# Local attention scores of 64 queries by 96 keys, and tiles placed at multiples of 512 bytes, in a fused sparse-attention and feed-forward kernel

## The chip, the cores and the metric

The kernel runs on one core of a Trainium2 chip. The metric is device time in microseconds for one execution of the whole program. Engines are named as in the profile: PE (TensorE), DVE (VectorE), ACT (ScalarE), POOL (GpSimd) and SP (SyncE, which issues DMAs).

## The reference

Inputs are q, k and v of 8 batches, 8 heads, 576 tokens and 64 dimensions, and two weight matrices, all float32. Heads 0 to 3 attend locally: a query sees itself and the 31 tokens before it. Heads 4 to 7 attend with stride 32: a query sees the earlier tokens at the same place modulo 32. The result goes through a feed-forward layer.

```python
scores = scale * np.matmul(q, k.transpose(0, 1, 3, 2))
mask_local = (rel >= 0) & (rel < stride)          # rel = query - key, stride = 32
mask_strided = (rel >= 0) & (pos[None, :] % stride == pos[:, None] % stride)
scores = np.where(masks[None, :, :, :], scores, -1000000000.0)
attn = softmax(scores)                            # over the keys
x = (attn @ v) as 4608 tokens of 512
h = x @ w_in                                      # 512 by 2048
out = (h * sigmoid(h)) @ w_out                    # 2048 by 512
```

## The kernel before

**The feed-forward part.** Tokens go in nine blocks of 512, the hidden dimension in 16 chunks of 128. Every float32 matrix product is made of three products of float32r values: each operand is split into a high and a low part (`xhi` and `xlo`, `ghi` and `glo`, and two weight tiles), and high by high, high by low and low by high are summed. So a chunk of the first layer (`hidden`, L594) is 12 matmul instructions of 128 x 128 by 512 columns with `w` stationary and `x` moving, and a chunk of the second (`output`, L658) is 12 with `g` stationary and the weights moving: 2 x 9 x 16 x 12 = 3,456 in all. Between the layers `silu` makes th (ACT, L604), the gate (DVE, L626), `ghi` (L634) and `glo` (L638).

The weights stay in SBUF. Of the second layer, chunks 0 to 6 lie in tiles named `w`; chunks 7 and 8 are lent the tiles `k2` and `k3`, chunks 9 to 11 the tiles `v2` to `v5`, and chunks 12 to 15 the `stage` tiles, once the first batch no longer needs these.

**The attention part.** Each batch has three local groups (12 tiles of 32 queries for each of two heads) and three strided ones (8, 8 and 6 tiles). Steps of a group: `scores` (PE, L378), `peak` (DVE, L396: scale, mask and running minimum into `sm`), `weigh` (ACT, L413: exponential and its sum), `total` (DVE, L428 and L429), `scale` (DVE, L432), `turn_by_blocks` (DVE, L454 and L457: transposes of 32 x 32 blocks from `sm` to `pt`), `values_by_halves` (PE, L497) and `done_by_halves` (ACT, L509 and L537). A local tile's scores are a product of 32 queries by 64 keys; a float32 product is two PE instructions.

**Order.** Up to the end of the first block everything follows an order written out by hand (`PLAN`). Each engine runs its instructions in that order. From then on a loop goes over chunks: `hidden` of one chunk, `silu`, and `output` of the chunk before. Three times per block (chunks 1, 6 and 11) `products` puts a burst on PE: local scores of a later group, local values, strided values, strided scores of a later group. Behind it stand the outstanding `output`, the local group's `weigh`, `normalize` and transposes, and three quarters of the strided `weigh`; the rest follows one and two chunks later. After a burst no output is outstanding, so the next chunk's gate must be done when the `hidden` behind it ends. Groups are counted over the batches, six a batch, local ones at even numbers from batch 1 on.

**Memory.** Tiles of the pool `const` come first in each partition, in the order in which they are made; the compiled program rounds each up to 32 bytes. `pad0` ends at byte 1,536, so the `v` tiles, `k` tiles and `ident` begin at multiples of 512. Then come four masks of 288 bytes, `ones` (8 bytes, rounded to 32) and `pad1` (376, rounded to 384): `stage0` begins at byte 38,432, which is 75 x 512 + 32, and everything behind it (stages, `w`, `xb`, `sm`, `pt`, `x`, `th`, `g`) is 32 bytes past a multiple too, but for the small `sums`.

POOL makes `ident` and the masks at the start, in program order.

Of the kernel before, what the change touches and what calls it, by code (L numbers as in the profile page):

```python
# [13 lines left out]
F32 = mybir.dt.float32  # L14
# [9 lines left out]
B, H, S, D = 8, 8, 576, 64  # L24
DM, DFF = 512, 2048
STRIDE = 32
NJ = S // STRIDE
NP = H // 2
P = 128
# [13 lines left out]


KW = 64
SEQ = 3 * NJ
QW = 512
HALF = SEQ // 2
# [16 lines left out]
class Group:  # L65
    def __init__(self, local, first, count):
        self.local, self.first, self.count = local, first, count
        self.rows = STRIDE if local else KW
        self.per = P // self.rows
        self.n = count // self.per  # L70
        self.q0 = [self.rows * t for t in range(count)]
        half = S // STRIDE
        gap = [STRIDE if local and first < half <= first + t else 0 for t in range(count)]
        self.k0 = [(STRIDE if local else SEQ) * t + g for t, g in enumerate(gap)]
        self.nq = self.q0[-1] + self.rows
        self.nk = self.k0[-1] + KW

        self.at = [(t % self.n, t // self.n) for t in range(count)]

        self.starts = [  # L80
            tuple(r for t, (at, r) in enumerate(self.at)
                  if at == c and local and (first + t) % half == 0)
            for c in range(self.n)
        ]
# [88 lines left out]
def sparse_attention_ffn(ctx: ExitStack, tc: tile.TileContext, kqt, vt, w_in, w_out, out):  # L173
    nc = tc.nc
    const = ctx.enter_context(tc.tile_pool(name="const", bufs=1))
# [26 lines left out]
    make_identity(nc, ident)  # L202


    def mask(name):
        m = const.tile([P, 72], F32, name=name)
        nc.gpsimd.memset(m, 0.0)
        return m

    def keep(m, p0, rows, shape, steps, base, channel):  # L210
        part = m[p0 : p0 + rows, : math.prod(shape)]
        nc.gpsimd.affine_select(
            out=part, in_=part, pattern=[[s, c] for s, c in zip(steps, shape)],
            base=base, channel_multiplier=channel, compare_op=ALU.is_ge, fill=NEG,
        )

    masks = {}
    m = mask("mask_local")
    for t in range(P // STRIDE):
        keep(m, t * STRIDE, STRIDE, [KW], [1], -1, -1)  # L220
        keep(m, t * STRIDE, STRIDE, [KW], [-1], STRIDE, 1)
    masks[True, ()] = m
    for starts in sorted({s for g in GROUPS for s in g.starts if s}):
        first = const.tile([P, 72], F32, name="mask_first" + "".join(map(str, starts)))
        nc.gpsimd.tensor_copy(out=first, in_=m)
        for t in starts:
            keep(first, t * STRIDE, STRIDE, [KW], [1], -STRIDE, 0)
        masks[True, starts] = first
# [5 lines left out]
    masks[False, ()] = m  # L234
    ones = const.tile([P, 2], F32, name="ones")
    nc.gpsimd.memset(ones, 0.0)
    for h in range(2):
        nc.gpsimd.memset(ones[h * D : (h + 1) * D, h : h + 1], 1.0)
    const.tile([P, 94], F32, name="pad1")


    cuts = ((0, NFC), (0, 7, 9, 12, 14, NFC))
# [102 lines left out]
    class Attention:  # L345


        def __init__(self, b, at):
            self.b, self.at, self.gi = b, at, order_of(b)[at]
            self.by_blocks = b * NG + at >= TURNED  # L350
            self.g = g = GROUPS[self.gi]
            self.spread = b * NG + at in SPREAD
            self.sums_by_pe = self.spread and g.local and not self.by_blocks
            self.kbd, self.vbd = kbds[kbd_of(b, at)], vbds[vbd_of(b, at)]
            self.cols = g.n * P
            self.tiles = [
                (t, c, slice(r * g.rows, (r + 1) * g.rows))
                for t, (c, r) in sorted(enumerate(g.at), key=lambda tile: tile[1])
            ]


# [5 lines left out]

        def halves(self, banks):

            return [t.rearrange("p (c k) -> p c k", k=KW)[:, : self.g.n] for t in banks]  # L370

        def scores(self, banks=None):
            g, kbd = self.g, self.kbd
            self.pss = banks or [self.bank("pss") for _ in range(2)]
            for t, c, rows in self.tiles:
                for h in range(2):
                    at = slice(h * D, (h + 1) * D)
                    nc.tensor.matmul(  # L378
                        self.pss[h][rows, c * KW : (c + 1) * KW],
                        kbd[at, 1, g.q0[t] : g.q0[t] + g.rows],  # L380
                        kbd[at, 0, g.k0[t] : g.k0[t] + KW], start=True, stop=True,
                    )

        def peak(self):
            g = self.g
            s_ps = self.halves(self.pss)
            self.sm = att.tile([P, 512], F32, name="sm", bufs=3)
            self.s_sb = self.sm.rearrange("p (c h k) -> p c h k", h=2, k=KW)[:, : g.n]
# [3 lines left out]
            self.inv = rsum.unsqueeze(3).broadcast_to([P, g.n, 2, KW])  # L392
            for c in range(g.n):
                for h in range(2):

                    nc.vector.tensor_tensor_reduce(  # L396
                        out=s_sb[:, c, h], in0=s_ps[h][:, c], in1=masks[g.local, g.starts[c]][:, :KW],
                        scale=-SCALE, scalar=BIG, op0=ALU.add, op1=ALU.min,
                        accum_out=peaks[:, c, h : h + 1],
                    )  # L400

        def lessen(self):
            peaks = self.peaks.unsqueeze(3).broadcast_to([P, self.g.n, 2, KW])
            nc.gpsimd.tensor_sub(self.s_sb, self.s_sb, peaks)

        def weigh(self, cs=None):
# [38 lines left out]
        def turn_by_blocks(self):  # L445

            n, size = self.g.n, P // STRIDE
            pt = att.tile([P, 512], F32, name="pt")[:, : self.cols]  # L450
            self.pt = pt = pt.rearrange("k (s c h q) -> k s c h q", s=2, h=2, q=STRIDE)
            src = self.sm[:, : self.cols].rearrange("p (c h s k) -> p s c h k", h=2, s=2, k=STRIDE)
            for s in range(2):
                nc.vector.transpose(out=pt[:, s], in_=src[:, s])  # L454
            for r in range(size):
                rows, to = (slice(i * STRIDE, (i + 1) * STRIDE) for i in (r, r ^ 1))
                nc.vector.transpose(out=pt[to, r % 2], in_=src[rows, 1 - r % 2])  # L457

        def values(self):
            g, pt, vbd = self.g, self.pt, self.vbd  # L460
# [26 lines left out]
        def values_by_halves(self, banks):  # L487
            g, pt, vbd = self.g, self.pt, self.vbd
            self.pso = banks
            half, size = g.count // 2, STRIDE if g.local else SEQ  # L490
            for i in range(half):
                for p in range(2):
                    c, r = g.at[p * half + i]
# [552 lines left out]
```

## Time and profile before

| | |
|---|---|
| median of 3 runs | 879.7 us (879.64 to 879.81) |
| the profiled execution | 879.54 us |
| its span | 877.6 us |
| PE busy | 869.5 us, 7217 matmul instructions |
| DVE, ACT, POOL busy | 509.4, 315.5, 37.2 us |
| granted PE clock | 1.0 of full speed |

The span runs from the first to the last instruction that the profiler saw; the time of the execution has 1.9 us more around it. An engine's share of busy time is a mean over stretches with different limits. Matmuls overlap in their pipeline, so the duration of one (some 390 ns for 512 columns) is longer than its distance to the next.

### The profile page before, as it was taken

To read this page: it belongs to the slowest core of one execution; us is meant where nothing else is said; L and a number is where in the kernel's file an instruction comes from. 1 tells how busy PE (TensorE), PEld (TensorE's weight loads), DVE (VectorE), ACT (ScalarE), POOL (GpSimd) and SP (SyncE) were. 2 spreads that over 40 slices of the span, in tenths; PEclk is the share of its full clock that TensorE was granted. 3 is DMA by queue.
4 is the path that set the end of the run, shared out by engine and by line. 5 is a ranking of instruction groups with operands and counts; after the bars stand their busy time and mean duration, and the time that the engine had idled before them with its cause. 6 is when DMAs were issued, how large, how long until landed. Compare 5 with 4: busy or idle time off the path is not lost.

```text
span 877.6 us, 18034 instructions
## 1 busy us (share of the span) xinstructions
PE 869.5 (99%) x7217; PEld 709.1 (81%) x7217; DVE 509.4 (58%) x1602; ACT 315.5 (36%) x1070; POOL 37.2 (4%) x55
## 2 busy tenths in 40 slices
PE   9999999999999999999999999999999999999998
PEld 6877788888878888888888888888888888888886
DVE  6999887448556646646645755664662533343333
ACT  7987763314412333333331441333331311131111
POOL 3123410000000000000000000000000000000000
PEclk9999999999999999999999999999999999999999
DMA  8976452202301212220320230221210000000001
GB/s 284 311 245 212 138 175 69 72 8 70 117 16 56 77 52 65 72 74 23 97 72 1 76 117 1 71 77 49 69 29 1 24 25 1 1 27 23 0 1 48
DMA packets 37044, 64.60 MB, mean 74 GB/s; under 512 B 2912, under 2 KB 23776, under 8 KB 36960
## 3 DMA queue, kind: packets, MB, share of 16 engines
q1 hardware_dynamic: 36144, 62.79, 21.9%
q8 instruction: 56, 0.92, 0.4%
q10 hardware_dynamic: 816, 0.66, 0.3%
q14 instruction: 28, 0.23, 0.1%
HBM read 54.00 MB, written 9.44 MB: 72 GB/s over the span
## 4 chain that ended last, share of the span: by engine, by line
PE 93%; DVE 2%; ACT 2%; DMA 1%; issue 1%; SPq 0%; POOL 0%; POOLq 0%; ACTq 0%; DVEq 0%
PE po L658 44%; PE ps L594 42%; PE ps L497 3%; PE ps L378 3%; PE ps L752 1%; DMA stage<-w_out 1%; DMA stage<-w_in 1%; ACT stage L265 1%; DVE stage L271 1%; ACT stage L260 0%; DVE glo L638 0%; DVE th L626 0%; ACT sm L413 0%; SPq L336 0%; DVE sm L396 0%
## 5 line engine op out<-in xcount | busy, mean ns | idle before, releaser
L594 PE MATMUL ps<-xhi,w 128*128 128x512 f32 x1152 | 377.2, 390 | 0.6 <-DVE th L626 0.6
L626 DVE SCALAR_TENSOR_TENSOR th<-th,ps 128x512 f32<-128x512 f32 (+1 forms) x147 | 99.2, 676 | 269.9 <-ACT th L604 269.8
L594 PEld LDWEIGHTS ps<-xhi,w 128*128 128x128 f32 x1152 | 216.2, 188 | 47.3 <-DVE th L626 0.9
L604 ACT ACTIVATE th<-ps 128x512 f32<-128x512 f32 (+1 forms) x147 | 86.6, 590 | 456.0 <-PE ps L594 453.3
L594 PE MATMUL ps<-xlo,w 128*128 128x512 f32 x576 | 224.5, 390 | 0.0
L658 PE MATMUL po<-w,ghi 128*128 128x512 f32 x504 | 157.1, 392 | 1.2 <-DVE sums L396 1.1
L594 PEld LDWEIGHTS ps<-xlo,w 128*128 128x128 f32 x576 | 108.1, 188 | 22.3
L658 PEld LDWEIGHTS po<-w,ghi 128*128 128x128 f32 x504 | 93.7, 188 | 21.2 <-issue 1.0
L413 ACT ACTIVATE sm<-sm,sums 128x64 f32<-128x64 f32 x320 | 106.4, 339 | 2.9 <-DVE sums L396 2.9
L638 DVE TENSOR_TENSOR glo<-th,ghi 128x512 fp32r<-128x512 f32 (+1 forms) x139 | 95.7, 688 | 11.9
L658 PE MATMUL po<-w,glo 128*128 128x512 f32 x252 | 98.4, 391 | 0.4 <-DVE glo L638 0.4
L658 PE MATMUL po<-stage,ghi 128*128 128x512 f32 x288 | 88.8, 389 | 0.0
L658 PE MATMUL po<-v,ghi 128*128 128x512 f32 x216 | 68.8, 400 | 0.0
L457 DVE STREAM_TRANSPOSE pt<-sm 32x192 f32<-32x192 f32 (+1 forms) x168 | 65.9, 392 | 3.0
L634 DVE CAST ghi<-th 128x512 fp32r<-128x512 f32 (+1 forms) x134 | 56.6, 422 | 12.9 <-PE po L658 1.3
L658 PEld LDWEIGHTS po<-stage,ghi 128*128 128x128 f32 x288 | 54.0, 188 | 11.2
L413 ACT ACTIVATION_READ_ACCUMULATOR sm<-sm,sums 128x1 f32 x320 | 61.7, 193 | 0.0
L658 PEld LDWEIGHTS po<-w,glo 128*128 128x128 f32 x252 | 47.3, 188 | 11.3 <-DVE glo L638 1.0
L658 PE MATMUL po<-stage,glo 128*128 128x512 f32 x144 | 56.0, 389 | 0.0
L658 PEld LDWEIGHTS po<-v,ghi 128*128 128x128 f32 x216 | 39.9, 188 | 9.3
L658 PE MATMUL po<-k,ghi 128*128 128x512 f32 x144 | 45.3, 396 | 0.0
L658 PE MATMUL po<-v,glo 128*128 128x512 f32 x108 | 42.7, 396 | 0.0
(75 smaller groups left out, 668.5 us busy)
## 6 DMA issues: line engine op xcount, KB each, us to landing
out<-stage SPq DMA_DIRECT2D x36, 256.0 KB, 2.1
v<-vt SPq DMA_DIRECT2D x21, 384.0 KB, 5.3
stage<-w_out SPq DMA_DIRECT2D x14, 512.0 KB, 4.1
k<-kqt SPq DMA_DIRECT2D x14, 512.0 KB, 5.2
stage<-w_in SPq DMA_DIRECT2D x12, 512.0 KB, 4.3
k<-kqt SPq DMA_DIRECT2D x14, 416.0 KB, 3.8
v<-vt SPq DMA_DIRECT2D x14, 256.0 KB, 5.2
k<-kqt SPq DMA_DIRECT2D x7, 448.0 KB, 4.1
```

The costliest lines, as they stand in the source:

```text
L265: nc.scalar.activation(out=lower, in_=lower.bitcast(U32), func=AF.Copy, scale=0.875 * 2.0**-29, bias=0.49)
L271: nc.vector.scalar_tensor_tensor(out=upper, in0=upper, scalar=3, in1=lower, op0=ALU.logical_shift_left, op1=ALU.bitwise_or,)
L378: nc.tensor.matmul(self.pss[h][rows, c * KW : (c + 1) * KW], kbd[at, 1, g.q0[t] : g.q0[t] + g.rows], kbd[at, 0, g.k0[t] : g.k0[t] + KW], s ...
L413: nc.scalar.activation(out=self.s_sb[:, c, h], in_=self.s_sb[:, c, h], func=AF.Exp, bias=self.peaks[:, c, h : h + 1], scale=-1.0, accum_ou ...
L457: nc.vector.transpose(out=pt[to, r % 2], in_=src[rows, 1 - r % 2])
L497: nc.tensor.matmul(self.pso[p][h * D : (h + 1) * D, i * size : (i + 1) * size], vbd[at, 2 * i + h], moved, start=True, stop=True,)
L594: nc.tensor.matmul(ph, weight(0, wi, fc)[:, cc * P : (cc + 1) * P], x[xi][cc], start=(cc, n) == (0, 0), stop=(cc, n) == (NP - 1, 2),)
L604: nc.scalar.activation(out=th[:, cols], in_=ph[:, cols], func=AF.Tanh, scale=0.5)
L626: nc.vector.scalar_tensor_tensor(out=th[:, cols], in0=th[:, cols], scalar=1.0, in1=ph[:, cols], op0=ALU.add, op1=ALU.mult,)
L634: copy[engine](out=g[0][:, cols], in_=th[:, cols])
L638: either[engine].tensor_sub(out=g[1][:, cols], in0=th[:, cols], in1=g[0][:, cols].bitcast(F32))
L658: nc.tensor.matmul(po[tt], g[gi][:, cols], weight(1, wi, fc), start=fc == 0 and n == 0, stop=fc == NFC - 1 and n == 2,)
```

## The change

Two things change. Groups from number 14 on (the second local group of batch 2 and all local groups after it) make their local scores in products of 64 queries by 96 keys: two neighbouring tiles share one product, whose keys are the block before the first, the first's own and the second's own. The tiles are laid out in pairs for that (`paired`), the masks have a form of 96 keys, `sm` has 640 columns, and the rows of `sm` hold 96 weights where they held 64; the transposes pick the two blocks of 32 that each tile needs. `values_by_halves` is as before but for the place of each tile. The PSUM bank shared by values and later scores is cut at column 192 for local groups. Second, `pad1` has 160 columns. By the same rounding, `stage0` then begins at byte 39,936, which is 78 x 512, and all tiles behind it begin at multiples of 512 (the `sums` at multiples of 128).

```diff
+WIDE = KW + STRIDE
+WIDE_FROM = 14
...
+        self.paired = [(t % (count // 2) // 2, 2 * (t // (count // 2)) + t % 2)
+                       for t in range(count)]
...
-    m = mask("mask_local")
-    for t in range(P // STRIDE):
-        keep(m, t * STRIDE, STRIDE, [KW], [1], -1, -1)
-        keep(m, t * STRIDE, STRIDE, [KW], [-1], STRIDE, 1)
-    masks[True, ()] = m
...
+    for wide, keys in ((False, KW), (True, WIDE)):
+        m = mask(f"mask_local{keys}", keys + 8)
+        for t in range(P // STRIDE):
+            ahead = STRIDE * (t % 2) if wide else 0
+            keep(m, t * STRIDE, STRIDE, [keys], [1], -1 - ahead, -1)
+            keep(m, t * STRIDE, STRIDE, [keys], [-1], STRIDE + ahead, 1)
+        masks[wide, ()] = m
+        some = {s for g in GROUPS for s in (g.paired_starts if wide else g.starts) if s}
+        for starts in sorted(some):
+            first = const.tile([P, keys + 8], F32, name=f"mask{keys}_" + "".join(map(str, starts)))
+            nc.gpsimd.tensor_copy(out=first, in_=m)
+            for t in starts:
+                keep(first, t * STRIDE, STRIDE, [keys], [1], -STRIDE, 0)
+            masks[wide, starts] = first
     m = mask("mask_strided")
...
-    const.tile([P, 94], F32, name="pad1")
+    const.tile([P, 160], F32, name="pad1")
...
+            self.wide = g.local and b * NG + at >= WIDE_FROM
+            self.at_of = g.paired if self.wide else g.at
+            self.keys = WIDE if self.wide else KW
...
+            if self.wide:
+                for t in (0, 6, 2, 8, 4, 10):
+                    c, r = self.at_of[t]
+                    rows = slice(r * STRIDE, (r + 2) * STRIDE)
+                    for h in range(2):
+                        at = slice(h * D, (h + 1) * D)
+                        nc.tensor.matmul(
+                            self.pss[h][rows, c * WIDE : (c + 1) * WIDE],
+                            kbd[at, 1, g.q0[t] : g.q0[t] + 2 * STRIDE],
+                            kbd[at, 0, g.k0[t] : g.k0[t] + WIDE], start=True, stop=True,
+                        )
+                return
...
-            self.sm = att.tile([P, 512], F32, name="sm", bufs=3)
+            self.sm = att.tile([P, 640], F32, name="sm", bufs=3)
...
+            blocks = self.keys // STRIDE
+            src = self.sm[:, : n * 2 * self.keys].rearrange(
+                "p (c h s k) -> p s c h k", h=2, s=blocks, k=STRIDE
+            )
             for s in range(2):
-                nc.vector.transpose(out=pt[:, s], in_=src[:, s])
+                nc.vector.transpose(out=pt[:, s], in_=src[:, s * (blocks - 1)])
...
-                nc.vector.transpose(out=pt[to, r % 2], in_=src[rows, 1 - r % 2])
+                nc.vector.transpose(out=pt[to, r % 2], in_=src[rows, 1 if self.wide else 1 - r % 2])
...
-            left, right = ([bank[:, at : at + 256] for bank in banks] for at in (0, 256))
+            cut = 192 if groups[i].g.local else 256
+            left, right = [bank[:, :cut] for bank in banks], [bank[:, cut:] for bank in banks]
```

## Rows read from the trace of the kernel before

**Rows 1.** The page: busy time by engine, and the chain's shares by line.
```profile
PE 869.5 (99%) x7217; PEld 709.1 (81%) x7217; DVE 509.4 (58%) x1602; ACT 315.5 (36%) x1070; POOL 37.2 (4%) x55
...
PE po L658 44%; PE ps L594 42%; PE ps L497 3%; PE ps L378 3%; PE ps L752 1%; DMA stage<-w_out 1%; DMA stage<-w_in 1%; ACT stage L265 1%; DVE stage L271 1%; ACT stage L260 0%; DVE glo L638 0%; DVE th L626 0%; ACT sm L413 0%; SPq L336 0%; DVE sm L396 0%
```

**Rows 2.** The chain of waits, 300 to 400 us: start us, us, work.
```profile
345.38 2.72 PE ps L594 x12
348.10 2.72 PE po L658 x12
...
366.98 2.80 PE po L658 x12
369.79 2.75 PE ps L594 x12
...
383.62 2.80 PE po L658 x12
```

**Rows 3.** Groups by shape: line, engine, tiles, count | busy us, mean ns | idle.
```profile
L658 PE MATMUL po<-w,ghi 128*128 128x512 f32 x504 | 157.1, 392 | 1.2 <-DVE sums L396 1.1
...
L658 PE MATMUL po<-stage,ghi 128*128 128x512 f32 x288 | 88.8, 389 | 0.0
L658 PE MATMUL po<-v,ghi 128*128 128x512 f32 x216 | 68.8, 400 | 0.0
...
L658 PE MATMUL po<-k,ghi 128*128 128x512 f32 x144 | 45.3, 396 | 0.0
```

**Rows 4.** PE's timeline over one burst: start us, us, work.
```profile
326.31 0.72 PE L378 MATMUL ps<-k 64*32 64x64 f32 x48
326.96 1.39 PE L497 MATMUL ps<-pt,v 64*64 64x32 f32 x80
328.17 0.66 PE L378 MATMUL ps<-k 64*64 64x64 f32 x32
328.75 0.72 PE L658 MATMUL po<-w,ghi 128*128 128x512 f32 x2
```

**Rows 5.** The chain of waits near the start.
```profile
11.71 0.33 PE po L438 x3
```

**Rows 6.** Groups by shape on ACT and DVE.
```profile
L413 ACT ACTIVATE sm<-sm,sums 128x64 f32<-128x64 f32 x320 | 106.4, 339 | 2.9 <-DVE sums L396 2.9
...
L432 DVE TENSOR_TENSOR sm<-sm,sums 128x384 f32<-128x384 f32 x27 | 17.2, 636 | 0.9
...
L432 DVE TENSOR_TENSOR sm<-sm,sums 128x512 f32<-128x512 f32 x13 | 9.0, 692 | 0.5
```

**Rows 7.** DVE's timeline behind the same burst.
```profile
332.17 0.56 DVE L432 TENSOR_TENSOR sm<-sm,sums 128x384 f32<-128x384 f32 x1
...
335.17 0.69 DVE L626 SCALAR_TENSOR_TENSOR th<-th,ps 128x512 f32<-128x512 f32 x1 [0.22 <-ACT th L604]
...
336.36 0.69 DVE L638 TENSOR_TENSOR glo<-th,ghi 128x512 fp32r<-128x512 f32 x1
```

**Rows 8.** PE's timeline where that output begins.
```profile
337.06 0.61 PE L658 MATMUL po<-w,ghi 128*128 128x512 f32 x2
337.51 0.39 PE L658 MATMUL po<-w,glo 128*128 128x512 f32 x1
```

**Rows 9.** POOL's timeline at the start.
```profile
1.02 0.29 POOL masks.py:199 TENSOR_SCALAR_AFFINE_SELECT ident<-ident 128x128 f32<-128x128 f32 x1
...
1.49 2.27 POOL L212 TENSOR_SCALAR_AFFINE_SELECT mask_local<-mask_local 32x64 f32<-32x64 f32 x8
3.82 0.24 POOL L225 COPY mask_first<-mask_local 128x72 f32<-128x72 f32 x1
...
4.32 0.23 POOL L225 COPY mask_first<-mask_local 128x72 f32<-128x72 f32 x1
...
5.14 2.46 POOL L212 TENSOR_SCALAR_AFFINE_SELECT mask_strided<-mask_strided 32x72 f32<-32x72 f32 x8
```

**Rows 10.** DVE's timeline at the first strided reduction.
```profile
11.00 0.22 DVE L396 CUSTOM_DVE_ANT_0 sm<-ps,mask_strided 128x64 f32<-128x64 f32 x1
```

More of the change, by code (lines that the diff above doesn't have):

```diff
@@ L78, in __init__ @@
         self.at = [(t % self.n, t // self.n) for t in range(count)]
[L80 to L84, printed above, removed]
+        self.paired = [(t % (count // 2) // 2, 2 * (t // (count // 2)) + t % 2)
+                       for t in range(count)]
+        self.starts, self.paired_starts = (
+            [tuple(r for t, (at, r) in enumerate(ats)
+                   if at == c and local and (first + t) % half == 0) for c in range(self.n)]
+            for ats in (self.at, self.paired)
+        )
 GROUPS = [Group(True, 12 * i, 12) for i in range(3)]
@@ L202, in sparse_attention_ffn, with mask @@
     make_identity(nc, ident)
-    def mask(name):
-        m = const.tile([P, 72], F32, name=name)
+    def mask(name, columns=72):
+        m = const.tile([P, columns], F32, name=name)
         nc.gpsimd.memset(m, 0.0)
@@ L217, in sparse_attention_ffn @@
     masks = {}
-    m = mask("mask_local")
-    for t in range(P // STRIDE):
-        keep(m, t * STRIDE, STRIDE, [KW], [1], -1, -1)
-        keep(m, t * STRIDE, STRIDE, [KW], [-1], STRIDE, 1)
-    masks[True, ()] = m
[L223 to L228, printed above, removed]
+    for wide, keys in ((False, KW), (True, WIDE)):
[12 more added lines that the diff above has]
+            masks[wide, starts] = first
     m = mask("mask_strided")
@@ L233, in sparse_attention_ffn @@
         keep(m, t * STRIDE, STRIDE, [4, NJ], [NJ, 0], NJ - 1 - q0, -1)
-    masks[False, ()] = m
+    masks[None, ()] = m
     ones = const.tile([P, 2], F32, name="ones")
@@ L355, in __init__ @@
             self.cols = g.n * P
+            self.wide = g.local and b * NG + at >= WIDE_FROM
+            self.at_of = g.paired if self.wide else g.at
+            self.keys = WIDE if self.wide else KW
+            starts = g.paired_starts if self.wide else g.starts
+            self.masks = [masks[self.wide if g.local else None, some] for some in starts]
             self.tiles = [
                 (t, c, slice(r * g.rows, (r + 1) * g.rows))
-                for t, (c, r) in sorted(enumerate(g.at), key=lambda tile: tile[1])
+                for t, (c, r) in sorted(enumerate(self.at_of), key=lambda tile: tile[1])
             ]
@@ L368, in halves @@
         def halves(self, banks):
-            return [t.rearrange("p (c k) -> p c k", k=KW)[:, : self.g.n] for t in banks]
+            n, keys = self.g.n, self.keys
+            return [t[:, : n * keys].rearrange("p (c k) -> p c k", k=keys) for t in banks]
         def scores(self, banks=None):
@@ L386, in peak @@
             s_ps = self.halves(self.pss)
-            self.sm = att.tile([P, 512], F32, name="sm", bufs=3)
-            self.s_sb = self.sm.rearrange("p (c h k) -> p c h k", h=2, k=KW)[:, : g.n]
+            self.sm = att.tile([P, 640], F32, name="sm", bufs=3)
+            self.s_sb = self.sm[:, : g.n * 2 * self.keys].rearrange(
+                "p (c h k) -> p c h k", h=2, k=self.keys
+            )
             s_sb = self.s_sb
@@ L391, in peak @@
             self.peaks, self.rsum = peaks, rsum = sums[:, 0, : g.n], sums[:, 1, : g.n]
-            self.inv = rsum.unsqueeze(3).broadcast_to([P, g.n, 2, KW])
+            self.inv = rsum.unsqueeze(3).broadcast_to([P, g.n, 2, self.keys])
             for c in range(g.n):
@@ L396, in peak @@
                     nc.vector.tensor_tensor_reduce(
-                        out=s_sb[:, c, h], in0=s_ps[h][:, c], in1=masks[g.local, g.starts[c]][:, :KW],
+                        out=s_sb[:, c, h], in0=s_ps[h][:, c], in1=self.masks[c][:, : self.keys],
                         scale=-SCALE, scalar=BIG, op0=ALU.add, op1=ALU.min,
@@ L402, in lessen @@
         def lessen(self):
-            peaks = self.peaks.unsqueeze(3).broadcast_to([P, self.g.n, 2, KW])
+            peaks = self.peaks.unsqueeze(3).broadcast_to([P, self.g.n, 2, self.keys])
             nc.gpsimd.tensor_sub(self.s_sb, self.s_sb, peaks)
@@ L451, in turn_by_blocks @@
             self.pt = pt = pt.rearrange("k (s c h q) -> k s c h q", s=2, h=2, q=STRIDE)
-            src = self.sm[:, : self.cols].rearrange("p (c h s k) -> p s c h k", h=2, s=2, k=STRIDE)
+            blocks = self.keys // STRIDE
+            src = self.sm[:, : n * 2 * self.keys].rearrange(
+                "p (c h s k) -> p s c h k", h=2, s=blocks, k=STRIDE
+            )
             for s in range(2):
-                nc.vector.transpose(out=pt[:, s], in_=src[:, s])
+                nc.vector.transpose(out=pt[:, s], in_=src[:, s * (blocks - 1)])
             for r in range(size):
                 rows, to = (slice(i * STRIDE, (i + 1) * STRIDE) for i in (r, r ^ 1))
-                nc.vector.transpose(out=pt[to, r % 2], in_=src[rows, 1 - r % 2])
+                nc.vector.transpose(out=pt[to, r % 2], in_=src[rows, 1 if self.wide else 1 - r % 2])
         def values(self):
@@ L492, in values_by_halves @@
                 for p in range(2):
-                    c, r = g.at[p * half + i]
+                    c, r = self.at_of[p * half + i]
                     at = slice(p * KW, (p + 1) * KW)
```

## The prediction

> **What bounds the kernel now.** I read the page first, then the chain of waits in the steady stretch, then the groups by shape, then single stretches of the timeline.
>
> The page shows PE at work for 99% of the span and on 93% of the chain; two lines carry it, the second layer's products (L658) and the first layer's (L594) [rows 1]. So the span is the number of PE instructions times their spacing, plus what the attention bursts insert, plus the start. What another engine does counts only where it is late for PE.
>
> The chain puts a time on twelve products, one chunk of one layer: 2.72 us where the weights lie in their own tiles, that is 226.7 ns for 512 columns. Where the moving weights lie in the lent `k` and `v` tiles the same twelve take 2.80 us, and the twelve after them 2.75 [rows 2]. Nothing else differs between these products in shape, and no engine is waited for; the groups by shape show the same thing as 396 and 400 ns against 389 and 392 for one [rows 3]. This is the only place in the steady stretch where an address can be seen in a time. In the program of before the `v`, `k` and `ident` tiles begin at multiples of 512 bytes, and everything allocated behind `pad1` (`stage`, `w`, `xb`, `sm`, `x`, `th`, `g`) begins 32 bytes past one. A product from `w` has both operands 32 bytes past; one from `k` or `v` has the moving operand at a multiple and the stationary `ghi`/`glo` 32 bytes past.
>
> A burst of attention sits between two chunks: local scores from 326.31 to 326.96, values to 328.17, strided scores to 328.75 [rows 4].
>
> **The change part by part.**
>
> *Local scores.* 17 groups change: two of batch 2, three of each of batches 3 to 7. Each now issues 48 PE matmul instructions (24 products, two instructions each) for 0.65 us [rows 4]; after it 24, of 64 x 64 array cells and 96 columns instead of 64 x 32 and 64. How long are they? The values, also 64 x 64 with 32 and 54 columns, run at 1.21 us for 80, 15.1 ns each [rows 4]; if 96 columns changed nothing, 24 would take 0.36 us. The other bound is that columns count: 128 columns of a float32 transpose take 0.33 us for three, 110 ns each or 0.86 ns a column [rows 5]; each quarter of the array gets three products, six instructions of 96 columns, 6 x 96 x 0.86 = 0.50 us, and some 0.03 to get going. I take 0.53, because 64 columns on four quarters already take 64 x 0.86 = 55 ns of the 4 x 15.1 = 60 that four instructions need, so there is no room to hide more columns. Halving the instructions is thus mostly eaten by longer ones. What is left is the change of tile shape between scores and values: 48 instructions at under 11 ns would be 0.51 us, and 0.65 are taken, so some 0.1 us passes before the values start; in the new form both are 64 x 64. Gain 0.12 us a group, 17 x 0.12 = **2.0 us**; bounds 17 x 0.05 = 0.9 and 17 x 0.29 = 4.9.
>
> *The masked minimum, weights, scaling.* On DVE six reductions a group grow from 64 to 96 columns, on ACT six exponentials (339 ns now), and on DVE the scaling grows from 384 to 576 elements [rows 6]. Slope: 128 more elements of the scaling cost 692 - 636 = 56 ns by the means, up to 1.06 ns an element by the single one here (0.56 us) against the 512-wide mean [rows 6, 7]; I take +0.2 us. The exponentials have no row at 96; by 0.85 to 1.1 ns an element they grow by some 30 ns, 0.18 us for six. The transposes move the same 192 columns. So the local chain ends some 0.4 us later relative to its scores, and those end 0.12 earlier. Who waits? On DVE the gate of the next chunk stands behind the transposes; it began at 335.17 after 0.22 us of idleness, `glo` began at 336.36 and ended at 337.05 [rows 7], and PE used it in the third product of the output, at 337.51, with its weight load one product earlier, near 337.29 [rows 8]. The cover is 0.22 us of DVE's idleness plus about 0.2 between `glo` and that load: 0.4 in all, just what the delay needs. I take nothing; with the cover gone it costs up to 0.2 us a group, 3.4 us. The strided scaling that follows on DVE is wanted only five chunks later.
>
> *Masks at the start.* POOL makes three more masks, and before the strided one. Eight selects of 64 columns took 2.27 us, copy and select for one first-mask 0.5 (3.82 to 4.32), the one select of 128 x 128 took 0.29 where a narrow one with its gap took 2.27 / 8 = 0.28, so width is cheap [rows 9]. At 96 columns I estimate 0.2 + 2.5 + 2 x 0.55 = 3.9 us. The strided mask, done at 7.60, is then done at about 11.5; DVE wants it at 11.00 [rows 9, 10]. The waiting instruction is the first strided reduction; behind it on DVE stand the copy of the turned weights, the sums and the sharing of the first groups, and for its banks the next scores on PE and then a `k` load on SP. 0.5 us late at most, in a stretch with idle filler on PE; I take **+0.3 us**, bounds 0 and 0.7.
>
> *Alignment.* After the change all tiles behind `pad1` begin at multiples of 512, as `k` and `v` do, so both operands of every product lie alike. I take it that what costs the `k` and `v` chunks is the 32 bytes between the two operands, since 45 chunks (five of sixteen, nine blocks; 540 instructions: the 216 + 144 with `ghi` are two of every three [rows 3]) differ from the rest in that, and that products of operands that lie alike take 226.7 ns wherever they lie. Then each of the 45 gives back 0.08 + 0.03 us [rows 2]: 45 x 0.11 = **4.9 us**. For the other 2,916 instructions I take no change, which no row of before can show: none has both operands at a multiple of 512. Bounds: 213.3 ns (512 columns at 2.4 GHz, the granted clock being full) and 233.3 (2.80 / 12).
>
> *The rest.* The cut of the PSUM bank at 192 instead of 256 moves only addresses. No DMA is added or moved; SP's order stays.
>
> Sum: 877.6 - 2.0 - 4.9 + 0.3 = 871.0 us of span. The profiled run took 879.54 us around 877.6 of span, 1.9 more, and stands 0.2 under the median: 871.0 + 1.9 + 0.1 = **873.0 us**.
>
> **The rivals.**
>
> *Slower: the multiple itself is what costs.* `k` and `v` differ from `w` also in that the moving tile begins at a multiple of 512. If that is the cause, the `k` and `v` chunks keep their time and the 2,916 other products get it: 2,916 x 6.7 ns = 19.5 us, 877.6 + 19.5 - 2.0 + 0.3 + 2.0 = 897.4 us. It decides from 1.7 us / 2,916 = 0.6 ns a product on. For it: the rows cannot tell it from mine, as the stationary operand is 32 bytes past throughout. Against it: after a `k` or `v` chunk the next twelve, with neither operand at a multiple, are also late by 0.03 us [rows 2], which looks like two streams that have lost step rather than like a slow address. The Trainium skill (TensorE: Matmul & The Clock Gate, Step-by-step: what each phase is for) says that PE reads the moving operand and the weights through two independent ports, so that the one takes nothing from the other; by that rule it could not be the distance between operands, and this rival would stand at 897.4. No row here decides it.
>
> *Much faster: the 226.7 are themselves a toll of the 32 bytes.* 512 columns at 2.4 GHz are 213.3 ns, so 13.4 ns a product are unexplained. If all go, 3,456 x 13.4 = 46.3 us more than in my sum: 826.7; a quarter of them, 861.4. For it: transposes whose moving operand `ident` lies at a multiple run at 110 ns for 128 columns, almost without a remainder over twice 53.3 [rows 5]. Against it: these have a slower stream of their own, so they say little. The Trainium skill (TensorE: Matmul & The Clock Gate, Back-to-back issue gap) gives about 216 ns for 512 columns; by that figure the estimate would be 3,456 x 10.7 = 37 us under my sum, 836.
>
> *No effect of addresses.* `k` and `v` keep 2.80 for some other reason, such as their place far from the other tiles: 877.6 - 2.0 + 0.3 + 2.0 = 877.9 us.
>
> *The gate is late.* With DVE's cover gone, 0.2 us a group: 876.4; within my own case's range.
>
> **How the numbers follow.** My case 0.55, own range 869.5 to 877 (score bounds, start, DVE); much or somewhat faster 0.17; no effect of addresses 0.15; slower 0.13. The range 862 to 881 holds my case and the third, the part of the second where up to a quarter of the toll goes (0.08) and little of the last: about 0.79. A change under 0.2% (1.8 us, so 877.9 to 881.5) cannot be told from none. Faster: 0.55 + 0.17 + half of 0.15 = 0.80; same 0.07; slower 0.13.
>
> **What would show it.** Right: in the chain every chunk takes 2.72 us, `k` and `v` too, and 2.72 behind them; the local scores run about 0.53 us as 24 instructions; no wait of PE for DVE some 9 us after a burst. Wrong: chunks of `w` at 2.80 (first rival), at 2.6 (second), or `k` and `v` still at 2.80 with `w` at 2.72 (third); PE idle before L658 on `glo` after each burst; the steady stretch beginning more than 0.7 us later than now, chunk for chunk.

## The result, and the profile after

The changed kernel took 871.5 us (median; 871.39 to 871.88), the one before on the same chip 879.7 (879.33 to 879.81): a ratio of 0.9909, 95% interval 0.9891 to 0.9926. The forecast was 873.0. The profiled execution took 871.88 us with a span of 870.1, 7.5 less than before, at a granted clock of 1.0 in both.

Line numbers have moved: the first layer's products are L623 (were L594), the second's L687 (L658), the wide local scores L393, the other scores L402, the values L526, the masked minimum L422 (L396), the scaling L458, the transposes L483 and L486, the gate L655, `glo` L667, the selects that make masks L215.

From the page of the changed kernel, the busy times; they answer to [rows 1]:

```profile
PE 862.5 (99%) x6809; PEld 707.9 (81%) x6809; DVE 514.1 (59%) x1602; ACT 318.7 (37%) x1070; POOL 40.3 (5%) x68
```

PE has 408 fewer matmul instructions, 17 groups of 24, and 7.0 us less to do; DVE and ACT have 4.7 and 3.2 us more. PE still bounds the kernel.

The chain of waits of the changed kernel, 300 to 400 us (start us, us, work), which answers to [rows 2] and, in its first four lines, to the burst of [rows 4]:

```profile
323.91 0.66 PE ps L393 x24
324.56 1.16 PE ps L526 x80
325.72 0.47 PE ps L402 x32
326.19 2.97 PE po L687 x12
...
345.48 2.72 PE po L687 x12
...
364.19 2.72 PE po L687 x12
366.92 2.72 PE ps L623 x12
...
380.51 2.72 PE po L687 x12
```

The pieces at 364.19 (weights in `k`) and at 380.51 (in `v`) now take the 2.72 us of the one at 345.48 (in `w`), and so do the twelve behind; they took 2.80 and 2.75. The groups by shape say the same: `k` has come down from 396 to 389 ns and `v` from 400 to 394, and `w` and `stage` stand where they stood [rows 3].

```profile
L687 PE MATMUL po<-w,ghi 128*128 128x512 f32 x504 | 156.9, 392 | 0.0
L687 PE MATMUL po<-stage,ghi 128*128 128x512 f32 x288 | 88.8, 389 | 0.0
L687 PE MATMUL po<-v,ghi 128*128 128x512 f32 x216 | 67.5, 394 | 0.0
...
L687 PE MATMUL po<-k,ghi 128*128 128x512 f32 x144 | 44.3, 389 | 0.0
```

The burst in PE's timeline of the changed kernel, by the start of its first instructions; it answers to [rows 4]:

```profile
323.84 0.72 PE L393 MATMUL ps<-k 64*64 64x96 f32 x24
324.38 1.34 PE L526 MATMUL ps<-pt,v 64*64 64x32 f32 x80
325.54 0.66 PE L402 MATMUL ps<-k 64*64 64x64 f32 x32
326.12 0.50 PE L687 MATMUL po<-w,ghi 128*128 128x512 f32 x1
```

From the first score to the first product behind the burst it is 326.12 - 323.84 = 2.28 us; it was 328.75 - 326.31 = 2.44. The 0.16 come from the local scores (0.54 instead of 0.65 until the values start) and, by 0.05, from the local values (0.67 instead of 0.72 by the starts of their instructions). The starts of single instructions say where: from the first score to the last it is 0.483 us instead of 0.508, from the last score to the first value 62 ns instead of 146, and from the first four values to the next four 28 ns instead of 79; the later steps between local values are 58 ns in both. It is the same in all 17 bursts. So 0.13 of the 0.16 lie where the scores pass over to the values, and the scores themselves, 24 instructions for 48, are 0.025 us shorter.

Where the 7.5 us of span went, worked out by laying the start of the same big product in one trace against its start in the other:

| | us |
|---|---|
| `k` and `v` chunks and those behind: 0.36 us in the first of nine blocks, 0.43 to 0.46 in six, 0.53 in the last two | -4.2 |
| ahead of the first `k` chunk: the first experiment's kernel (below; tiles alike, old scores) is 0.33 earlier there than the one before, and the third's as well; what does it is not shown | -0.3 |
| 17 bursts, 0.16 each | -2.7 |
| single waits of PE at 262 and 550 us that the changed kernel does not have | -1.4 |
| start: 1.25 behind the first experiment's kernel, which has no new masks, at 106 us, 0.6 of it one wait of PE | +1.2 |
| behind the last product: the last write of the result lands 3.19 us after that product's start instead of 3.34 | -0.1 |
| sum | -7.5 |

### The profile page after: what moved, and what is told of

Read it like the earlier page. It is cut to its first block, busy times and chain, and to the rows that moved or that the text cites. A ratio compares the mean times of both kernels' runs of the same rounds, so it can differ in the third digit from the quotient of the medians.

```text
span 870.1 us, 17241 instructions
## 1 busy us (share of the span) xinstructions
PE 862.5 (99%) x6809; PEld 707.9 (81%) x6809; DVE 514.1 (59%) x1602; ACT 318.7 (37%) x1070; POOL 40.3 (5%) x68
## 4 chain that ended last, share of the span: by engine, by line
PE 92%; DVE 3%; ACT 2%; issue 1%; POOL 1%; POOLq 0%; DVEq 0%; ACTq 0%
PE po L687 44%; PE ps L623 43%; PE ps L526 3%; PE ps L393 1%; PE ps L402 1%; DVE stage L277 1%; DVE sm L422 1%; ACT stage L271 0%; ACT stage L266 0%; POOL mask_local L215 0%; DVE th L655 0%; DVE w L318 0%; ACT xb L566 0%; DVE w L322 0%; ACT sm L439 0%
## 5 line engine op out<-in xcount | busy, mean ns | idle before, releaser
L623 PE MATMUL ps<-xhi,w 128*128 128x512 f32 x1152 | 376.7, 390 | 0.5 <-DVE th L655 0.5
L623 PEld LDWEIGHTS ps<-xhi,w 128*128 128x128 f32 x1152 | 216.2, 188 | 46.0 <-DVE th L655 0.7
L655 DVE SCALAR_TENSOR_TENSOR th<-th,ps 128x512 f32<-128x512 f32 (+1 forms) x147 | 99.2, 675 | 258.6 <-ACT th L633 257.7
L623 PE MATMUL ps<-xlo,w 128*128 128x512 f32 x576 | 224.2, 389 | 0.0
L687 PE MATMUL po<-w,ghi 128*128 128x512 f32 x504 | 156.9, 392 | 0.0
L623 PEld LDWEIGHTS ps<-xlo,w 128*128 128x128 f32 x576 | 108.1, 188 | 22.2
L439 ACT ACTIVATE sm<-sm,sums 128x64 f32<-128x64 f32 (+1 forms) x320 | 109.2, 348 | 2.9 <-DVE sums L422 2.9
L687 PEld LDWEIGHTS po<-w,ghi 128*128 128x128 f32 x504 | 93.7, 188 | 20.0 <-DVE w L322 0.3
L667 DVE TENSOR_TENSOR glo<-th,ghi 128x512 fp32r<-128x512 f32 (+1 forms) x139 | 95.7, 689 | 11.9
L687 PE MATMUL po<-w,glo 128*128 128x512 f32 x252 | 98.4, 390 | 0.4 <-DVE glo L667 0.4
L687 PE MATMUL po<-stage,ghi 128*128 128x512 f32 x288 | 88.8, 389 | 0.0
L486 DVE STREAM_TRANSPOSE pt<-sm 32x192 f32<-32x192 f32 (+1 forms) x168 | 65.8, 392 | 3.0
L687 PE MATMUL po<-v,ghi 128*128 128x512 f32 x216 | 67.5, 394 | 0.0
L687 PEld LDWEIGHTS po<-stage,ghi 128*128 128x128 f32 x288 | 54.0, 188 | 11.2
L687 PEld LDWEIGHTS po<-w,glo 128*128 128x128 f32 x252 | 47.3, 188 | 11.1 <-DVE glo L667 1.1
L687 PE MATMUL po<-stage,glo 128*128 128x512 f32 x144 | 56.0, 389 | 0.0
L687 PEld LDWEIGHTS po<-v,ghi 128*128 128x128 f32 x216 | 39.9, 188 | 8.4
L687 PE MATMUL po<-k,ghi 128*128 128x512 f32 x144 | 44.3, 389 | 0.0
L687 PE MATMUL po<-v,glo 128*128 128x512 f32 x108 | 42.0, 389 | 0.0
```

Of the source, the lines that this page charges most:

```text
L439: nc.scalar.activation(out=self.s_sb[:, c, h], in_=self.s_sb[:, c, h], func=AF.Exp, bias=self.peaks[:, c, h : h + 1], scale=-1.0, accum_ou ...
L486: nc.vector.transpose(out=pt[to, r % 2], in_=src[rows, 1 if self.wide else 1 - r % 2])
L623: nc.tensor.matmul(ph, weight(0, wi, fc)[:, cc * P : (cc + 1) * P], x[xi][cc], start=(cc, n) == (0, 0), stop=(cc, n) == (NP - 1, 2),)
L655: nc.vector.scalar_tensor_tensor(out=th[:, cols], in0=th[:, cols], scalar=1.0, in1=ph[:, cols], op0=ALU.add, op1=ALU.mult,)
L667: either[engine].tensor_sub(out=g[1][:, cols], in0=th[:, cols], in1=g[0][:, cols].bitcast(F32))
L687: nc.tensor.matmul(po[tt], g[gi][:, cols], weight(1, wi, fc), start=fc == 0 and n == 0, stop=fc == NFC - 1 and n == 2,)
```

## The experiments

**1 to 3: where tiles begin.** The first is the kernel before with its later tiles at multiples of 512 and nothing else changed; the second the changed kernel with its later tiles 32 bytes past again; in the third, again the kernel before, all tiles begin 32 bytes past a multiple, `k`, `v` and the rest alike.

The first, against the kernel before; the third has this and `pad0` at 104 columns instead of 96:

```diff
-    const.tile([P, 94], F32, name="pad1")
+    const.tile([P, 88], F32, name="pad1")
```

The second, against the changed kernel:

```diff
-    const.tile([P, 160], F32, name="pad1")
+    const.tile([P, 168], F32, name="pad1")
```

> The kernel before with only the last pad changed (94 to 88 columns), so that every tile behind it begins at a multiple of 512 bytes, like the k and v tiles. My theory (a product is slow when its two operands lie differently): the 45 chunks whose weights lie in k and v fall from 2.80 to 2.72 us and the chunk behind each from 2.75 to 2.72, 45 x 0.108 = 4.9 us, 874.8 us in all. Since the PE instructions are those of before in number and order, PE's two odd waits before L658 at 262 us (1.1 us) and 550 us (0.24 us) stay. Rival (the alignment is worth nothing by itself and the new scores made the gain): 879.7 us.

> The changed kernel with its last pad at 168 columns, so that the tiles behind it begin 32 bytes past a multiple of 512 again. My theory: the k and v chunks are back at 2.80 us; 17 bursts shorter by 0.16 us give 2.7, the later start by the new masks takes 0.7 to 0.9 back, and the two odd waits of before (1.3 us in all) are gone if they hang on how many PE instructions come before them: 879.7 - 2.7 + 0.8 - 1.3 = 876.5 us; 877.8 if they do not hang on that. Rival (the scores gave all of the gain): 871.5 us.

> The kernel before with every tile, the k and v tiles too, 32 bytes past a multiple of 512. If the distance between the two operands is what counts: as with all tiles at multiples, 874.8 us, every chunk 2.72 us. If multiples of 512 are what counts: the k and v chunks stay at 2.80, or slower, 879.7 us or more.

Measured beside a kernel before of 879.8: the first 875.15 us (ratio 0.9949, 0.9936 to 0.9961), the second 875.8 (0.9955, 0.9942 to 0.9967), the third 875.4 (0.9949, 0.9937 to 0.9962). Each half of the change gives about half of the gain. The chains of waits tell why. The second experiment's, at the chunks of `k`:

```profile
364.93 2.80 PE po L687 x12
367.73 2.75 PE ps L623 x12
370.48 2.80 PE po L687 x12
```

The third's, at the same place:

```profile
365.63 2.72 PE po L658 x12
368.35 2.72 PE ps L594 x12
371.07 2.72 PE po L658 x12
```

The old 2.80 and 2.75 are back with 32 bytes between the operands. With no tile of these products at a multiple of 512 the third kernel is as fast as the first: to the products a multiple is worth nothing by itself. Alike is what counts. A multiple does show behind the last product: in every kernel whose later tiles lie 32 bytes past one (before, second, third) the span ends 4.28 to 4.30 us after the start of that product, in all others 4.14 to 4.16.

**4: the masks.** The changed kernel, with the masks of 96 keys made behind the strided mask and `ones` instead of ahead of them.

```diff
-    for wide, keys in ((False, KW), (True, WIDE)):
+    def local_masks(wide, keys):
...
+    local_masks(False, KW)
     m = mask("mask_strided")
...
+    local_masks(True, WIDE)
     const.tile([P, 160], F32, name="pad1")
```

> The changed kernel with the masks of 96 keys made on POOL behind the strided mask and the ones instead of ahead of them. My theory: the first strided reduction is back at 11.0 us, and the 0.5 to 0.9 us by which the start came later are won back: 870.6 to 871.0 us. Rival (the later start is hidden by the DMAs that the first weights wait for): 871.5 us, unchanged.

Measured 870.4 us (870.3 to 871.3; ratio 0.9892, 0.9877 to 0.9907), a little under what was expected, with a span of 869.5, 0.6 less than the changed kernel's. The first product of the first layer starts at 25.86 us instead of 26.32, and from 175 us on every product is 0.56 earlier. The first strided reduction no longer waits for its mask, but it starts at 11.41 us and not at 11.0 as expected (10.69 in a second profile of the same program). How much of it is the masks is taken up again below.

**5 and 6: how far apart.** The changed kernel with `v` and `k` moved: 64 and 128 bytes past a multiple in the fifth, 256 and 32 in the sixth. `ident` and the masks, which stand behind `k`, move with it; all tiles behind `pad1` are at multiples. `pad2` stands between the `v` and the `k` tiles.

```diff
-    const.tile([P, 96], F32, name="pad0")
+    const.tile([P, 112], F32, name="pad0")
...
+    const.tile([P, 16], F32, name="pad2")
...
-    const.tile([P, 160], F32, name="pad1")
+    const.tile([P, 128], F32, name="pad1")
```

That is the fifth; the sixth has 160, 72 and 152 columns in these three places.

> The changed kernel with the v tiles 64 bytes and the k tiles 128 bytes past a multiple of 512, everything else at multiples. If the distance between the two operands costs whatever its size, v chunks and k chunks both take 2.80 us again and the twelve products behind 2.75: 870.1 + 4.9 = 875.0 us of span. If the cost grows with the distance, 64 bytes would cost 0.16 us a v chunk (2.88) and 128 bytes 0.32 a k chunk (3.04): span about 880. If only distances below a block of 64 bytes cost, all stay at 2.72: span 870.1.

> The changed kernel with the v tiles 256 bytes and the k tiles 32 bytes past a multiple of 512, everything else at multiples. The k chunks now have the moving operand 32 bytes past and the stationary one at a multiple, the other way round than before. If the distance counts regardless of sign, the k chunks take 2.80 us; if it counts only when the stationary operand lies further on, they stay at 2.72. The v chunks, half a multiple away: 2.80 if any distance costs the same, more if it grows. Span 870.1 (nothing costs) to 875.0 (both cost as before).

One execution each, 874.5 and 873.6 us, with spans of 872.7 and 871.8. The chain of waits of the fifth (its lines are one further on); `k` is at 364.54, `v` at 375.59:

```profile
364.54 2.79 PE po L688 x12
367.33 2.73 PE ps L624 x12
...
375.59 2.76 PE po L688 x12
378.36 2.77 PE ps L624 x12
```

The same of the sixth, `k` at 364.45 and `v` at 375.57:

```profile
364.45 2.80 PE po L688 x12
367.25 2.76 PE ps L624 x12
...
375.57 2.72 PE po L688 x12
378.29 2.72 PE ps L624 x12
```

By the starts of the chunks, one and the twelve behind it take 5.44 us when alike. At 32 bytes they take 5.56 on this side and 5.55 on the other (2.80 + 2.75 before); at 64 and at 128 bytes 5.53, at 256 bytes 5.44 again. So the sign hardly matters, which the sixth's expectation allowed for, and the cost does not grow with the distance but shrinks a little and is gone at half of 512. None of the expectations had that; that only distances under 64 bytes count is refuted as well.

**7: the order of the local scores.** Three products in a row on the same half of the array's columns.

```diff
-                for t in (0, 6, 2, 8, 4, 10):
+                for t in (0, 2, 4, 6, 8, 10):
```

> The changed kernel with the six pairs of local scores in the order 0, 2, 4, 6, 8, 10, so that three products in a row go to the same half of the array's columns. Theory that each quarter of the array streams its own columns (six instructions of 96 columns at 0.86 ns): two quarters wait while two work, a block of scores takes about 1.0 us instead of 0.55, and the time is 17 x 0.45 = 7.7 us more, 879.2 us. Rival, that instructions are issued at some 21 to 23 ns whatever quarter they use: the block stays at 0.55 us and the time at 871.5.

Measured 875.0 us (874.91 to 875.27; ratio 0.9950, 0.9934 to 0.9967): 3.5 us more than the changed kernel, half of what the one theory says and not the nothing of the other. Of PE's timeline in this burst:

```profile
324.75 0.78 PE L393 MATMUL ps<-k 64*64 64x96 f32 x20
325.29 0.25 PE L526 MATMUL ps<-pt,v 64*64 64x32 f32 x2
325.36 0.24 PE L393 MATMUL ps<-k 64*64 64x96 f32 x1
...
325.46 1.27 PE L526 MATMUL ps<-pt,v 64*64 64x32 f32 x70
```

The starts of single instructions tell it apart. In the changed kernel four scores start within 20 ns, one for each quarter, at 323.971, 324.053, 324.136, 324.218 and 324.301 us: every 82.5 ns, and 96 columns at the 0.86 ns of the transposes [rows 5] are 82.6. In the reordered kernel two start together, at 324.882, 324.964 and 325.047, again 82.5 apart, but the other half's first pair already starts at 324.977, before the first half is through. So a quarter does stream its columns, as the theory has it; what it lacked is that PE gets on with later instructions for a free quarter (even the first values start ahead of the last scores), so that only part of the second half's time is added: the last score starts 0.70 us after the first, instead of 0.48. The rival, a rate of issue whatever the quarter, is refuted.

**8: the single waits of PE.** The kernel before had two that its neighbours in the order do not have: 1.1 us, put down to DVE's sums [rows 3], after the burst at 262 us, and a short one at 550. The first experiment still has both (1.1 us between two starts at 260.8, 0.7 at 547.1), the third the one at 260.8 (1.6); the second, fourth and seventh, with fewer PE instructions, have neither. This is the first experiment's kernel with its filler, products of `ident` with itself at the start whose results nothing reads, cut into more pieces: 30 PE instructions more.

```diff
-k0 k1 k2 k3 v0 ~9 S0 M0 k4 v1 E0 ~1 S1 k5 M1 E1 v2 ~1 S2 M2 E2 R0 ~2 T0 P0.D p0 S3 M3 E3 ~3 T1
+k0 k1 k2 k3 v0 ~1 ~1 ~1 ~1 ~1 ~1 ~1 ~1 ~1 S0 M0 k4 v1 E0 ~1 S1 k5 M1 E1 v2 ~1 S2 M2 E2 R0 ~1 ~1 T0 P0.D p0 S3 M3 E3 ~1 ~1 ~1 T1
...
```

> The kernel before with its tiles at multiples of 512 (as in the first experiment), and with each filler of n products in the written order split into n fillers of one: the same filler work in more pieces. Theory that the two odd waits of PE (about 0.9 us at 261 and 0.5 at 547) hang on the position in PE's own instruction stream: they move or vanish, and the time is between 873.8 and 875.2 us. Rival, that PE really waits there for DVE's sums: they stay at the same bursts, and the time is 875.2.

Measured 876.95 us (875.85 to 878.47; ratio 0.9973, 0.9963 to 0.9983), 1.8 more than the first experiment, where up to 1.4 less, or no change, was expected. The profiled execution was the longest of these. The waits at 261 and 547 us are gone, and there is another, at the end of a burst where no other kernel has one; PE's timeline:

```profile
518.67 0.53 PE L378 MATMUL ps<-k 64*64 64x64 f32 x23
520.46 0.38 PE L378 MATMUL ps<-k 64*64 64x64 f32 x9 [1.25 <-issue]
```

It falls between two scores of one group, where PE waits for no engine. At the start PE also has waits that end with nothing but the issue; of its list of waits (engine, line, released by: us in total, times, longest; the 1.3 is the one at 519 us):

```profile
PE ps L752 <- issue: 2.3, 1, 2.3
...
PE ps L378 <- issue: 1.3, 1, 1.3
PE po L477 <- issue: 0.7, 1, 0.7
```

The first product of the first layer starts 3.1 us later than in the first experiment, most of the 3.6 by which the span of this execution is longer. So the waits move when PE's instructions move. That they are not DVE's the three kernels with one at 261 or 262 us show too: the product behind it starts 0.09 us (first experiment), 0.31 (before) and 0.61 (third) after DVE's first sum of those strided scores, so it is not that sum which lets it go. But the place in PE's stream is not all of it: the third experiment has the first's instructions in the first's order, and no wait at 547 us. Around the wait at 519 us, 517.5 to 519.2, the list of DMA queues (packets, MB, share of 16 engines) has one transfer of a queue that carries instructions:

```profile
q8 instruction: 1, 0.02, 4.7%
```

The list of the kernel before has one too around its wait at 262 us, from 260.8 to 262.2:

```profile
q8 instruction: 1, 0.02, 4.1%
```

There are 56 of these in a run of the kernel before and 53 after the change. Their number follows PE's instructions (products, weight loads and those of its sequencer) in every trace: 56 for 14,529 (before, first, third), 53 for 13,617 or 13,713 (all with the new scores), 57 for the eighth's 14,590, that is one for 256 to 259. So they most likely bring PE's instructions, and that PE waits for one now and then fits. But nearly all of the 56 pass without a wait of PE, and why these few do not stays open.

**9 to 12: wide scores from two groups earlier, and three kernels on one chip.** The ninth is the fourth with two more groups of local scores in the wide form; the tenth is the changed kernel, the eleventh the fourth's and the twelfth the ninth's again.

```diff
-WIDE_FROM = 14
+WIDE_FROM = 10
```

> The changed kernel with the masks of 96 keys made behind the strided mask (as in the fourth experiment), and the local scores of 64 by 96 from two local groups earlier on (from group 10). If each such group gives back 0.16 us, as in the 17 others, the time is 0.3 us under the fourth experiment, 870.1 us; if those two groups' bursts lie where PE has cover by filler or waits for something else, nothing comes of it, 870.4.

> The changed kernel, on one chip with the next two: 871.5 us as before, and the start as in its first profile (first hidden product at 26.3 us).

> The kernel of the fourth experiment, on the same chip as the changed one: if what its profile gained at the start (0.46 us at the first hidden product, 0.56 of span) is the whole of it, 0.6 us less than the changed kernel; if the 1.1 us between the medians of two chips was real, 1.1 less.

> The kernel of the ninth experiment on the same chip: by the spans (869.3 against 869.5) 0.2 us less than the one with the late masks alone; if the two earlier groups give back 0.16 each, 0.3 less; if the medians of two chips were right, 0.8 more.

The ninth took 871.2 us (871.04 to 871.6; ratio 0.9911, 0.9895 to 0.9928). On one chip: changed 871.7 (871.36 to 872.01; ratio 0.9911, 0.9896 to 0.9925), late masks 870.9 (870.15 to 872.3; 0.9905, 0.9889 to 0.9922), late masks and two more groups 871.4 (870.88 to 872.21; 0.9909, 0.9894 to 0.9923). The second is 0.8 us under the first, but their runs overlap; it beats the changed kernel twice by the median and by less than one run differs from the next. The third was expected 0.2 or 0.3 under the second, or 0.8 above it, and came 0.6 above. The two earlier groups give nothing that shows: PE's wait for the first gate grows to 0.8 and 0.9 us there, from 0.5 and 0.6 with the late masks alone.

The profiles say why this can't be settled closer. They agree from 175 us on and differ ahead of that: the same program with late masks is 0.76 us earlier in the eleventh run than in the fourth, and the twelfth 1.1 later than the ninth. Of the waits of PE in the changed kernel's first profile:

```profile
PE po L511 <- issue: 0.6, 1, 0.6
PE po L573 <- DVE xq L550: 0.5, 2, 0.4
PE ps L623 <- DVE th L655: 0.5, 1, 0.5
```

And in the eleventh's:

```profile
PE ps L627 <- DVE th L659: 0.6, 1, 0.6
PE po L691 <- DVE glo L671: 0.4, 1, 0.4
PE po L577 <- DVE xq L554: 0.4, 1, 0.4
```

The waits that end with the issue come and go: 0.6 in the changed kernel's profile, 0.6 twice in the tenth, 0.5 in the fourth, 0.4 in the seventh, 0.8 and 0.3 in the twelfth, none in the second, the ninth and the eleventh. Taking these out of the time by which a kernel lies behind the first experiment at 106 us, ahead of the first wide score (135.1), leaves 0.65, 0.2 and 0.5 us for the three with the masks made early (changed, tenth, seventh) and 0.2 and -0.1 for the two with late masks. The second experiment, against the kernel before, gives 0.3.

## Why the prediction was right, step by step

**Alignment: right in cause, over in size.** Every chunk takes 2.72 us, and the other products stay at 226.7 ns, as taken. The 45 chunks give back 4.2 us by the traces, not 4.9: the term gave each of them 0.11 us, 0.08 for itself and 0.03 for the twelve behind. But where a burst falls among the five of a block, the chunk ahead of it has no twelve behind it and gave 0.08, and the one right behind it gave 0.06 (2.85 us to the start of the next twelve instead of 2.90). Another 0.3 came at the start, for which there was no term, so that alignment stands at 4.5 in all (the first experiment's span is 4.6 under the one before).

**The slower rival** fell with the first and third experiments: to these products the multiple costs nothing and brings nothing. The Trainium skill (TensorE: Matmul & The Clock Gate, Step-by-step: what each phase is for) has PE read its two operands through independent ports, which spoke for this rival; the third experiment, 2.72 us for every chunk with all tiles moved alike, beside the 2.80 of the kernel before, shows that here the place of one against the other does count, by 3% of a product.

**The much faster rival** fell too: 226.7 ns stayed in every kernel, with operands at multiples, at 32 bytes past and half a multiple apart. What the 13.4 ns over 512 columns are stays open. **No effect of addresses** fell with the first experiment, 4.6 us from one pad.

**Local scores: right in kind, under in size.** The block was put at 0.53 us and took 0.54, by the mechanism named: columns streamed by each quarter at 0.86 ns, 82.5 ns for 96. But the gain is 0.16 us a group, not 0.12, 2.7 us and not 2.0. The prediction put the gain down to the change of tile shape between scores and values, some 0.1 us; there the pause went from 146 to 62 ns, 0.08 us, and the scores themselves gave 0.025. What it had not is that the first step between the values shrinks as well, from 79 to 28 ns, the other 0.05; it left their length as it was. That scores of the values' own tile shape come ahead of them now fits both steps; shape and order were not tried apart.

**DVE and ACT: right.** DVE's timeline of the changed kernel behind the burst at 323.84, which answers to [rows 7]:

```profile
329.70 0.76 DVE L458 TENSOR_TENSOR sm<-sm,sums 128x576 f32<-128x576 f32 x1
...
332.71 0.69 DVE L655 SCALAR_TENSOR_TENSOR th<-th,ps 128x512 f32<-128x512 f32 x1
...
333.89 0.69 DVE L667 TENSOR_TENSOR glo<-th,ghi 128x512 fp32r<-128x512 f32 x1
```

The scaling is 0.2 us longer (0.76 for 0.56), as taken, and an exponential of 96 columns takes 367 ns for 339, the 30 more that were estimated. The gate has lost its 0.22 us of idleness, and starts 332.71 - 323.84 = 8.87 us after the burst's first score, 8.86 before; `glo` 10.05 after it in both. The idle time took up the delay, the 0.2 behind `glo` was not needed, and PE's list of waits has no gate in it but two of the start, which the list of before has as well.

**Masks: right in size, but not the whole start.** The selects of the strided mask end at 11.71 us (11.5 was forecast), and the first strided reduction waits for them. POOL's timeline, which answers to [rows 9]:

```profile
5.19 2.51 POOL L215 TENSOR_SCALAR_AFFINE_SELECT mask_local<-mask_local 32x96 f32<-32x96 f32 x8
...
9.20 2.51 POOL L215 TENSOR_SCALAR_AFFINE_SELECT mask_strided<-mask_strided 32x72 f32<-32x72 f32 x8
```

DVE's, which answers to [rows 10]:

```profile
11.74 0.22 DVE L422 CUSTOM_DVE_ANT_0 sm<-ps,mask_strided 128x64 f32<-128x64 f32 x1 [1.08 <-POOL mask_strided L215]
```

0.7 us late instead of at most 0.5, and 0.2 to 0.65 by 106 us, against 0.3 taken and 0 to 0.7 allowed. With late masks the same reckoning gives 0.2 and -0.1, so what the masks alone cost is not settled between profiles that differ by as much.

**What the prediction did not see: PE's single waits.** It counted PE instructions by their spacing and took the 1.2 us of idleness in [rows 3] as part of the kernel. 1.4 us of such waits went, at 262 and 550 us, and 0.6 came at the start. The span ended 0.9 us under the forecast of 871.0: -0.7 (bursts), -1.4 and +0.6 (single waits), +0.4 (alignment), +0.3 (masks), and -0.1 (the last writes), for which no term stood. These are 3.5 us of errors that leave 0.9: that the forecast came so close is in part luck. The other 0.6 of the 1.5 us between forecast and median lie outside the span: the median stands 1.4 us above the profiled span, not 2.0.

## What to carry to other kernels

Where groups of equal products differ by some per cent in their mean time, lay the addresses of both operands beside them before looking for a wait: here one pad was worth 4.6 us, and it was the distance between the operands, not a multiple, that counted. Fewer and wider instructions paid little by themselves here, 0.025 us a burst, since the array's parts already streamed nearly all the time; cost them by the columns of each part, spread them over the parts in turn, and look at what happens where one tile shape follows another, which gave the other 0.13. A single wait of the bounding engine that the trace lays to another engine, and that neighbours in the same loop don't have, may go or come with a change of the instruction count, so don't put it down to what the change was made for.

## What the runs showed of the hardware that was not expected

- Products of 512 columns took 226.7 ns when both operands lay alike to a multiple of 512 bytes, or half of 512 apart. At 32 bytes apart, twelve and the twelve behind took 0.11 to 0.12 us more, at 64 and at 128 bytes 0.09. Why 32 costs most and 256 nothing stays open.
- PE starts an instruction for a free part of the array while earlier ones wait for a busy part: in the seventh experiment the first values started at 325.294 us, ahead of the last scores at 325.447.
- From 64 x 32 scores to 64 x 64 values 146 ns passed between two starts, from 64 x 64 scores to the same values 62 ns.
- Single waits of PE of 0.2 to 2.3 us came and went when its instructions moved, and, at the start above all, from one run to the next. The 16 KB transfers of instructions that lie near them number one for 256 to 259 of PE's instructions; why a few of them come with a wait stays open.
